# K of the last four head pairs: transposed by the DMA crossbar instead of TensorE

## Chip, cores, metric

One Trainium2 chip, one core. The metric is the device time of one execution in microseconds (us), lower is better. Medians are over repeated executions; all executions quoted here were of the same (fast) state. A profiled span is about 1.7 us shorter than the device time of the same execution, so spans are compared with spans and times with times.

## The reference, cut

Attention with a selection of key chunks, then a gated MLP with a spatial mixing step. Batch 4, 8 heads, sequence 768, head size 64; float32 in and out.

```python
# attention: per head, chunks of 32 keys; upper bound of q.k per chunk from the chunk's min and max of K
ub     = sum_d max(q * k_min[chunk], q * k_max[chunk])     # [B, H, 768, 24], causal chunks only
top    = the 6 chunks with the largest ub
scores = q @ k.T / 8, masked to the chosen chunks and to j <= i
x      = softmax(scores) @ v                               # heads side by side: [4, 768, 512]
# MLP
h    = relu(x @ w_in);  u, v = halves of h
v    = layernorm(v);    v = w_spatial @ v + b_spatial
out  = (u * v) @ w_out                                     # [4, 768, 512]
```

## The kernel before

The 32 heads are worked as 16 pairs (`i` = 0 to 15), two heads side by side in the 128 partitions, so K of a pair is a 128 x 768 tile after transposition. All steps of all pairs and of the four MLPs are put on a list of "beats"; a scheduler of the language then orders each engine's instructions by their dependences. The MLP of one batch element runs interleaved with the attention of the next.

K takes this way. It is loaded for two pairs at once by GpSimd (POOL) into a tile `k` that has three buffers, transposed, reduced per chunk to max and min (`kmm`, on VectorE), and copied into the operand of the score matmuls (`kh`, on VectorE):

```python
def load_k(g, hi, xy=None):                       # pairs 2g and 2g+1
    ...
    tiles["k", g] = sb.tile([P, 2, NQT, 2, D], F16, tag="k", name="k", bufs=3)
    ...
    nc.gpsimd.dma_start(out=t[:, :, :, 1 - hi, :]..., in_=source(k, b, h, 2))

def k_transpose(self):
    if self.i < 16:                               # in this kernel: always
        self.kT = kT = ps_ml.tile([P, S], F16, tag="mlp", name="kTp")       # PSUM
        for t in range(NQT):                      # 6 blocks of 128 x 128
            nc.tensor.transpose(kT[:, t * P:(t + 1) * P], self.k[:, t], identity)
    else:
        self.kT = sb.tile([P, S], F16, tag="kT", name="kT", bufs=3)         # SBUF
        nc.sync.dma_start_transpose(out=self.kT.rearrange("d (t s) -> d t s", s=P),
                                    in_=self.k.rearrange("p t h d -> p (t h d)"))
def k_max(self):
    nc.vector.tensor_reduce(self.kmm[:, 0, :], self.kT..., op=Alu.max)
def k_operand(self, hi):
    copy(self.kh[hi][d0:d1], self.kT[d0:d1])      # nc.vector.tensor_copy
```

Four more things share queues with this. SyncE (SP) issues all the crossbar transposes: of the attention output (`xT<-x`), of the selected queries from pair 8 on (`a<-qs`), of the gated MLP rows (`gT<-g`), and the output stores. POOL issues all loads and also does the causal mask of the exponentiated scores (`e<-e`) that the values matmuls read:

```python
def triangle(self, hi):
    nc.gpsimd.affine_select(out=blk, in_=blk, compare_op=Alu.is_ge, fill=0.0, ...)   # on e
def values(self, hi, blocks, ...):
    mm(self.av[:, qi, :], lhsT=self.e[hi][:, c:c + P], rhs=self.v[hi][:, t, 0:D + 1], ...)
def normalise(self, hi):                          # frees the one accumulator of the values
    nc.vector.reciprocal(rec, self.av[:, :, D:D + 1])
    nc.vector.tensor_tensor(self.x16[:, :, hi, :], in0=self.av[:, :, 0:D], in1=rec..., op=Alu.mult)
```

SP and POOL each work through their instructions in order. An instruction that waits holds up all that stand behind it (below, a load of POOL that waited 13.06 us held up the mask behind it).

The softmax here doesn't subtract the row's maximum and nothing guards it: scores larger than these inputs give would overflow.

## Time and profile before

| | before |
|---|---|
| median, range | 208.66 us (208.53 to 208.81) |
| profiled span | 206.9 us |
| PE busy | 187.8 us, 91% |
| PE busy from 78 to 160 us | 82.0 of 82 us |
| last matmul starts | 202.63 us |

The page of the kernel before: busy time by engine, then rows of 40 slices of the span; each digit is the busy share of a slice in tenths, and PEclk the TensorE clock that was granted.

```profile
span 206.9 us, 5068 instructions
PE 187.8 (91%) x1922; PEld 115.1 (56%) x1922; DVE 154.5 (75%) x454; ACT 158.1 (76%) x326; POOL 80.5 (39%) x100
...
PE   0368999898899999999999999999999999999992
...
PEclk9999999999999999999999999999999999999999
```

From the twelfth slice on, TensorE is busy for 90% or more of each slice (9), up to the last one. The view of busy time by stretch says the same with more figures; after each engine's busy time stand its instructions, then the granted clock (1.00 is full), the DMA share and GB/s.

```profile
core 0: us, PE busy (x) PEld busy (x) DVE busy (x) ACT busy (x) POOL busy (x), PEclk, DMA share, GB/s
60.00:70.00 10.00, 9.73 (x119) 6.47 (x117) 9.75 (x31) 8.38 (x17) 3.92 (x5) 1.00 2.02 154
70.00:78.00 8.00, 7.65 (x93) 5.23 (x93) 7.24 (x27) 7.22 (x18) 5.47 (x6) 1.00 1.50 103
78.00:83.00 5.00, 5.00 (x50) 2.95 (x48) 4.97 (x11) 4.79 (x12) 1.33 (x2) 1.00 3.58 128
...
100.00:130.00 30.00, 30.00 (x310) 17.73 (x307) 26.56 (x83) 26.83 (x61) 6.62 (x7) 1.00 1.09 143
```

So a TensorE instruction that is taken away between 78 and 160 us should be a gain, and a wait of TensorE put in there should be a loss that nothing later gives back.

The timeline of POOL (start, duration, then what it is; in brackets the idle time before it and what ended it):

```profile
59.65 2.09 POOL L327 DMA_DIRECT2D k<-in_k_dram  x2
61.69 0.94 POOL L278 TENSOR_SCALAR_AFFINE_SELECT e<-e 128x768 f16<-128x768 f16 x1
66.06 0.86 POOL L278 TENSOR_SCALAR_AFFINE_SELECT e<-e 128x768 f16<-128x768 f16 x1 [3.44 <-ACT e L271]
...
76.43 2.02 POOL L327 DMA_DIRECT2D k<-in_k_dram  x2 [1.80 <-PE kTp L170]
```

The K load of pairs 12 and 13 is issued at 59.65 us; the last one, of pairs 14 and 15, at 76.43 us, when TensorE has transposed the K that lay in the buffer (`kTp`). The mask of pair 5's second head, at 66.06 us, stands between them. TensorE needs that mask at 70.44 us, when it loads it as weights (timeline of the weight loads):

```profile
70.44 0.44 PEld L289 LDWEIGHTS <-e 128*128 128x128 f16 x6
```

The removed work itself, from the query for the tile `kTp` (duration min/median/max in ns, then first and last start):

```profile
L170 PE MATMUL kTp<-identity,k x96: 216/219/314, 5.7 to 135.9; 128*128 128x128 f16 x96
L194 DVE COPY kh<-kTp x30: 508/556/562, 15.8 to 140.9; 64x768 f16<-64x768 f16 x30
L178 DVE TENSOR_REDUCE kmm<-kTp x16: 924/953/958, 6.6 to 136.2; 128x24 f16<-128x768 f16 x16
```

One transpose takes 219 ns from start to end, but they are pipelined and start 55 ns apart, and that is what one costs a full TensorE.

### The profile page before, as it was taken

What the parts mean: (1) busy time and instruction counts of PE and PEld (TensorE: products, weight loads), DVE (VectorE), ACT (ScalarE), POOL (GpSimd) and SP (SyncE); (2) the same over time, 40 slices, a digit from 0 to 9 for tenths busy, and PEclk for the clock granted to TensorE, in tenths of its full rate; (3) what the DMA queues carried; (4) which work ended last, traced back from release to release, by engine and by line L of the source; (5) the groups of instructions that cost most, each with busy time, mean ns of one, the idle gap of its engine ahead of it and who ended that gap; (6) DMA issues with size and microseconds to landing.
All of it is one profiled execution on the core that took longest, in us unless ns stands there. A gap on an engine that the chain in (4) does not pass through costs nothing.

```text
span 206.9 us, 5068 instructions
## 1 busy us (share of the span) xinstructions
PE 187.8 (91%) x1922; PEld 115.1 (56%) x1922; DVE 154.5 (75%) x454; ACT 158.1 (76%) x326; POOL 80.5 (39%) x100
## 2 busy tenths in 40 slices
PE   0368999898899999999999999999999999999992
PEld 0266776775666665656655656565555454444440
DVE  6467979989799989899797999887647456365520
ACT  4797989899998889785989996669999830666042
POOL 7997659596992463236114111111111110000000
PEclk9999999999999999999999999999999999999999
DMA  5999999999999999979998926648782124540356
GB/s 38 92 118 154 140 178 158 173 177 167 177 162 162 97 119 128 135 130 147 149 278 153 180 62 57 127 88 158 181 166 65 38 29 92 187 152 3 72 128 256
DMA packets 114424, 27.27 MB, mean 132 GB/s; under 512 B 109536, under 2 KB 110816, under 8 KB 114400
## 3 DMA queue, kind: packets, MB, share of 16 engines
q0 software_dynamic: 76544, 12.20, 89.8%
q1 hardware_dynamic: 37856, 14.75, 36.4%
q8 instruction: 15, 0.25, 0.5%
q14 instruction: 9, 0.07, 0.1%
HBM read 24.38 MB, written 6.29 MB: 148 GB/s over the span
## 4 chain that ended last, share of the span: by engine, by line
PE 69%; ACT 17%; DVE 8%; issue 2%; DMA 2%; POOL 0%; DVEq 0%; ACTq 0%; POOLq 0%
PE mlp L388 40%; PE sc L266 12%; ACT e L271 10%; PE acc L289 7%; PE kTp L170 2%; ACT a L257 2%; DVE kmm L178 2%; PE ub L222 2%; DMA k<-in_k_dram 2%; PE trm L251 2%; ACT vraw L398 1%; PE tr L205 1%; DVE vn L412 1%; DVE kmm L182 1%; ACT u L420 1%
## 5 line engine op out<-in xcount | busy, mean ns | idle before, releaser
L271 ACT ACTIVATE e<-sc 128x512 f16<-128x512 f32 x192 | 96.9, 553 | 14.8 <-PE sc L266 13.4
L266 PE MATMUL sc<-a,kh 128*128 128x512 f16 (+3 forms) x256 | 65.5, 308 | 2.1 <-ACT e L271 1.5
L388 PE MATMUL mlp<-w_in_sb,xT 128*128 128x512 f16 x192 | 53.0, 379 | 0.1
L278 POOL TENSOR_SCALAR_AFFINE_SELECT e<-e 128x768 f16<-128x768 f16 x24 | 20.9, 869 | 66.3 <-ACT e L271 66.3
L289 PEld LDWEIGHTS <-e 128*128 128x128 f16 x672 | 31.4, 97 | 17.0 <-DVE x L297 3.8
L388 PE MATMUL mlp<-vn,wsT 128*128 128x512 f16 x144 | 37.3, 379 | 0.0
L289 PE MATMUL acc<-vt,e 128*128 128x65 f16 x672 | 35.3, 193 | 0.7 <-DVE x L297 0.4
L266 PEld LDWEIGHTS <-kh 128*128 128x128 f16 x256 | 22.7, 98 | 13.3 <-issue 0.8
L437 ACT COPY o<-mlp 128x512 f32<-128x512 f32 x24 | 14.1, 586 | 19.5 <-PE mlp L388 19.1
L400 DVE BATCH_NORM_STATS2 stats<-vraw 128x6 f32<-128x512 f32 x24 | 16.6, 693 | 12.9 <-ACT vraw L398 12.5
L388 PE MATMUL mlp<-w_out_sb,gT 128*128 128x512 f16 x96 | 25.1, 379 | 0.0
L388 PEld LDWEIGHTS <-xT 128*128 128x128 f16 x192 | 17.2, 97 | 12.6 <-issue 0.4
L427 DVE SCALAR_TENSOR_TENSOR g<-mlp,b_col,u 128x512 f16<-128x512 f32 x24 | 17.9, 748 | 7.3 <-PE mlp L388 6.2
L232 DVE MAX8 max<-ub 128x8 f32<-128x8 f32 (+4 forms) x160 | 15.6, 165 | 5.1 <-PE ub L222 4.9
L388 PEld LDWEIGHTS <-wsT 128*128 128x128 f16 x144 | 12.9, 98 | 10.4
L178 DVE TENSOR_REDUCE kmm<-kTp 128x24 f16<-128x768 f16 x16 | 15.2, 948 | 3.7 <-PE kTp L170 2.7
L297 DVE TENSOR_TENSOR x<-acc,rec 128x384 f16<-128x384 f32 x32 | 17.6, 551 | 0.4
L336 POOL DMA_DIRECT2D qs<-in_q_dram x14 | 14.6, 1049 | 5.9 <-PE sc L266 5.9
L194 DVE COPY kh<-kTp 64x768 f16<-64x768 f16 x30 | 16.5, 549 | 0.5
L398 ACT ACTIVATE vraw<-mlp 128x512 f32<-128x512 f32 x24 | 14.4, 601 | 3.0 <-PE mlp L388 3.0
L420 ACT ACTIVATE u<-mlp 128x512 f16<-128x512 f32 x24 | 14.3, 598 | 1.7 <-PE mlp L388 1.5
L327 POOL DMA_DIRECT2D k<-in_k_dram x14 | 14.4, 1045 | 2.5 <-PE kTp L170 1.8
(67 smaller groups left out, 230.2 us busy)
## 6 DMA issues: line engine op xcount, KB each, us to landing
out_dram<-o SPq DMA_DIRECT2D x24, 256.0 KB, 2.3
vt<-in_v_dram POOLq DMA_DIRECT2D x8, 384.0 KB, 8.8
k<-in_k_dram POOLq DMA_DIRECT2D x14, 192.0 KB, 8.1
qs<-in_q_dram POOLq DMA_DIRECT2D x14, 192.0 KB, 7.5
ws_raw<-in_moe_w_spatial_dram POOLq DMA_DIRECT2D x6, 192.0 KB, 6.9
w_in_sb<-in_moe_w_in_dram POOLq DMA_DIRECT2D x8, 128.0 KB, 6.9
w_out_sb<-in_moe_w_out_dram POOLq DMA_DIRECT2D x4, 128.0 KB, 7.9
k<-in_k_dram POOLq DMA_DIRECT2D x4, 96.0 KB, 3.4
```

The lines of the kernel that those rows point to most:

```text
L178: nc.vector.tensor_reduce(self.kmm[:, 0, :], self.kT.rearrange("d (c ch) -> d c ch", ch=CHUNK), axis=AX.X, op=Alu.max)
L194: copy(self.kh[hi][d0:d1], self.kT[d0:d1])
L266: mm(sc[:, col:col + n], lhsT=self.kh[hi][:, t * P:(t + 1) * P], rhs=self.a[:, q0 // P:(q0 + n) // P, hi, :], start=True, stop=not diag)
L271: nc.scalar.activation(out=self.e[hi][:, g * 512:g * 512 + width], in_=sc[:, 0:width], func=Act.Exp, scale=scale)
L278: nc.gpsimd.affine_select(out=blk, in_=blk, compare_op=Alu.is_ge, fill=0.0, base=0, channel_multiplier=-1, pattern=[[0, NQT], [1, P]])
L289: mm(self.av[:, qi, :], lhsT=self.e[hi][:, c:c + P], rhs=self.v[hi][:, t, 0:D + 1], start=first and n == 0, stop=last and n == len(blocks) ...
L297: nc.vector.tensor_tensor(self.x16[:, :, hi, :], in0=self.av[:, :, 0:D], in1=rec.to_broadcast([P, NQT, D]), op=Alu.mult)
L388: mm(st[group][:, 0:cols], lhsT=lhsT, rhs=rhs, start=(j == 0), stop=(j == n - 1))
L398: nc.scalar.activation(st["vraw"][:, ti, :], h, func=Act.Relu)
L400: nc.vector.bn_stats(stats, st["vraw"][:, ti, :])
L420: nc.scalar.activation(st["u"][:, ti, :], h, func=Act.Relu)
L427: nc.vector.scalar_tensor_tensor(g, in0=vs, scalar=b_col[:, ti:ti + 1], in1=st["u"][:, ti, :], op0=Alu.add, op1=Alu.mult)
```

## The change

The intent is to take 24 transposes (four pairs of six) off the engine that bounds the kernel, and to give them to the crossbar of the DMA path, which the kernel already uses for three other transpositions. The branch was in the code already; only its limit moves.

```diff
         def k_transpose(self):
-            if self.i < 16:
+            if self.i < 12:
                 self.kT = kT = ps_ml.tile([P, S], F16, tag="mlp", name="kTp")
                 for t in range(NQT):
                     nc.tensor.transpose(kT[:, t * P:(t + 1) * P], self.k[:, t], identity)
```

## The prediction

> **What bounds the kernel now.** From about 76 us to the last matmul at 202.7 us TensorE streams without gaps: the table by stretches has PE busy 10.00 of 10 us nearly everywhere, and matmuls start as fast as their columns allow (216 ns per 512 columns, 55 ns per 128-column transpose). All start-to-start slack from 80 us on adds up to about 1.6 us. Before 76 us ScalarE, VectorE and the loads share the limit (DMA 99% busy in the page's slices).
>
> **What the change removes.** 24 PE transposes, in four groups at 104.06, 114.76, 125.06 and 135.65 us (timeline): 24 x 55 ns = 1.3 us of a saturated PE. On VectorE the K copies (556 ns from PSUM) may get cheaper; the reductions (950 ns) hardly. VectorE is not the limit there.
>
> **What it adds.** Four crossbar transposes on the SP queue: by the like xT<-x transposes 1.2 us of issue, 2.7 us to landing on a quiet queue, over 8 us on a full one.
>
> **What it moves.** This decides it. The instruction order of the two built programs differs before 104 us. The K transposes are no longer tied to PE's place in the program, so the scheduler puts those of pairs 12, 13 and 14 on SP directly behind the first xT transpose (60.87 us before), and the last K load (pairs 14, 15) now reuses the buffer of pairs 12, 13. On POOL its first half is queued ahead of the triangle mask that ran at 66.06 us before, and it waits for both crossbar transposes of pairs 12 and 13. Those wait for the K load that lands at 70.96 us (issued 60.67, 10.3 us). The Trainium skill, "DMA: Bandwidth & Descriptors", section "Anatomy of one DMA", says that DMA engines do not wait on semaphores, the issuing sequencer does; this trace agrees (POOL sat idle 1.80 us before the K load at 76.43, until kTp).
>
> So, estimated from these durations: load landed 71.0; two transposes issued to 73.5, second landed about 75.0; POOL issues the load (1.03 us), masks (0.87 us): done about 77.0. PE loads its weights from that masked tile at 70.44 us in the old trace and runs in order: a hole of about 6.6 us, against a PE that is full afterwards.
>
> SP then holds up the transpose of pair 14, and behind it xT and the first A transpose, until about 82 us. A should land near 91 us; PE needs it at 87.14 + 6.6 = 93.8, so no second hole.
>
> **Clock.** The skill, "TensorE: Matmul & The Clock Gate", Part 1, says that an idle window of about 3.4 us halves the clock and a busy one restores it. Here early transposes start 107 ns apart, later ones 55 ns, which agrees. I add 1.7 us (0 to 3.4).
>
> **Sum.** 208.7 + 6.6 + 1.7 - 1.3 - 0.7 (slack between 70 and 76 us absorbed) = 215.0 us. Range 211.5 to 218. Chances: faster 0.04, same 0.13, slower 0.83.
>
> **What would show it.** PE idle 5 to 8 us near 70 to 77 us, its weight load (values, acc<-vt,e) released by the POOL mask; POOL idle there, released by the DMA kT<-k; slices of PEclk below 9 just after; first xT then three kT on SP, the third near 82 us; no kTp group after 95 us; PE gapless from about 85 us to the end, that stretch about 1.3 us shorter.
>
> **What would make it wrong.** The K load landing earlier, or quicker transposes: a smaller hole. A clock that stays up. A late A transpose: a second hole near 90 us. If POOL doesn't block, 207.4 us.

## The result

| | before | change |
|---|---|---|
| median, range | 208.74 us (208.53 to 209.19), 4 runs | 218.75 us (217.92 to 219.71), 4 runs |
| ratio, 95% interval | | 1.048 (1.0448 to 1.0513): slower |
| profiled span | 206.9 us | 217.0 us |
| mean granted clock | 1.000 | 0.974 |
| last matmul starts | 202.63 us | 212.28 us |

Ratios here and below are the mean time of one kernel's fast runs over that of the other's of the same rounds on the same chip, so not quite the ratio of the medians.

The page of the change:

```profile
span 217.0 us, 5030 instructions
PE 189.6 (87%) x1898; PEld 115.1 (53%) x1898; DVE 155.6 (72%) x454; ACT 158.7 (73%) x326; POOL 80.4 (37%) x100
...
PE   0479998988999069999999899999999999999992
...
PEclk9999999999999658999999999999999999999998
```

There is one slice in which TensorE is idle (0), and the clock falls with it (6, 5, 8). PE's busy time even rises, though it has 24 instructions fewer, since matmuls at half clock last longer. The same stretches as before:

```profile
60.00:70.00 10.00, 9.73 (x119) 6.49 (x117) 9.75 (x31) 8.37 (x17) 2.55 (x3) 1.00 1.99 159
70.00:78.00 8.00, 1.21 (x14) 0.72 (x14) 0.81 (x3) 1.20 (x3) 2.39 (x3) 0.66 0.37 57
78.00:83.00 5.00, 5.00 (x34) 3.08 (x32) 3.81 (x8) 3.02 (x8) 3.96 (x5) 0.53 1.91 122
...
100.00:130.00 30.00, 28.23 (x286) 16.10 (x284) 29.05 (x85) 25.37 (x58) 10.00 (x10) 1.00 1.36 163
```

Three losses can be read here. Up to 70 us TensorE does the same. From 70 to 78 us TensorE does 14 matmuls in place of 93. From 78 to 83 us it is "busy" but does 34, in place of 50, at a clock of 0.53. And from 100 to 130 us it does 286 in place of 310, with VectorE now at 29.05 of 30 us. (The change runs some 10 us late there, so the stretch doesn't hold the same work in both; that TensorE is busy for 28.23 us and no longer for 30.00 is the safer sign.)

**The hole.** POOL in the change, timeline:

```profile
59.58 2.09 POOL L327 DMA_DIRECT2D k<-in_k_dram  x2
61.61 0.94 POOL L278 TENSOR_SCALAR_AFFINE_SELECT e<-e 128x768 f16<-128x768 f16 x1
75.61 1.03 POOL L327 DMA_DIRECT2D k<-in_k_dram  x1 [13.06 <-DMA kT<-k]
76.64 0.88 POOL L278 TENSOR_SCALAR_AFFINE_SELECT e<-e 128x768 f16<-128x768 f16 x1
```

The last K load now stands ahead of the mask and waits for the crossbar transposes of pairs 12 and 13, whose buffer it reuses. POOL sits idle for 13.06 us, and the mask comes at 76.64 instead of 66.06 us. SP in the change, timeline; the line with x3 spans three issues, at 70.63, 71.90 and 81.70 us, with landings at 73.41, 74.75 and 88.19 us:

```profile
60.84 1.77 SPq L305 DMA_TRANSPOSE xT<-x  x1
70.63 12.29 SPq L173 DMA_TRANSPOSE kT<-k  x3
82.97 1.40 SPq L305 DMA_TRANSPOSE xT<-x  x1
```

The first of them waited for the load of K, which was issued at 60.59 and landed at 70.55 us. And the weight loads of TensorE:

```profile
70.14 0.15 PEld L388 LDWEIGHTS <-xT 128*128 128x128 f16 x2
77.58 0.35 PEld L289 LDWEIGHTS <-e 128*128 128x128 f16 x6 [7.28 <-POOL e L278]
```

So the chain is: K load landed, two transposes on SP, K load on POOL, mask on POOL, TensorE. Measured by the starts of the matmuls, the hole adds 6.95 us at 70.41 us.

**The clock.** The records of the granted clock show 0.5 from 72.50 to 82.74 us, in all 10.24 us. Of these about 5.2 us lie after the hole, with TensorE at work at half speed: a loss of about 2.6 us in this execution, worked out from those times.

**Later gaps.** From 100 us on there are new holes in TensorE's stream, of 0.40, 0.33, 1.15 and 0.54 us (105.18, 116.30, 120.84 and 127.81 us). Each stands before a values matmul that waits for the accumulator, that is for VectorE's normalisation (`x`). VectorE in the change around the largest, timeline:

```profile
116.70 0.94 DVE L178 TENSOR_REDUCE kmm<-kT 128x24 f16<-128x768 f16 x1
...
118.16 0.93 DVE L182 TENSOR_REDUCE kmm<-kT 128x24 f16<-128x768 f16 x1
...
120.38 0.18 DVE L296 RECIPROCAL rec<-acc 128x6 f32<-128x6 f32 x1
120.59 1.10 DVE L194 COPY kh<-kT 64x768 f16<-64x768 f16 x1
121.61 0.53 DVE L297 TENSOR_TENSOR x<-acc,rec 128x384 f16<-128x384 f32 x1
```

A K copy of 1.10 us stands between the reciprocal and the product of one normalisation, and TensorE waits for the product. With `kT` ready early, the work on K of pairs 12 to 15 is no longer held back by TensorE, and stands earlier and closer together in VectorE's order. The kernel before has no such gap between 74 and 160 us.

What the K work costs from its new place, from the query for the tile `kT`:

```profile
L194 DVE COPY kh<-kT x8: 331/358/1096, 102.5 to 138.2; 64x768 f16<-64x768 f16 x8
L173 SPq DMA_TRANSPOSE kT<-k x4: 1214/1240/1282, 70.6 to 115.7; - x4
L178 DVE TENSOR_REDUCE kmm<-kT x4: 931/936/952, 110.9 to 125.0; 128x24 f16<-128x768 f16 x4
```

The copies take 358 ns instead of 556 at the median, but three of the eight took 820, 1005 and 1096 ns. Each of these three ran while POOL was at work on a mask or a load issue, and ended 0.15 to 0.22 us after POOL's instruction, while the other five met no instruction of POOL (the 1096 ns one at 121.69 us, after a load issue from 120.11 to 121.54 us). That one held up the other is read from these times; no run separates it. The reductions hardly differ (936 and 953 ns); this agrees with the Trainium skill, "VectorE: DVE Perf Modes", section "Rules for kernel authors", which says to expect no faster mode from a `tensor_reduce`.

### The profile page after: what moved, and what is told of

It is laid out like the page before. It is cut to its first block, busy times and chain, and to the rows that moved or that the text cites. A ratio compares the mean times of both kernels' runs of the same rounds, so it can differ in the third digit from the quotient of the medians.

```text
span 217.0 us, 5030 instructions
## 1 busy us (share of the span) xinstructions
PE 189.6 (87%) x1898; PEld 115.1 (53%) x1898; DVE 155.6 (72%) x454; ACT 158.7 (73%) x326; POOL 80.4 (37%) x100
## 4 chain that ended last, share of the span: by engine, by line
PE 58%; ACT 13%; DVE 12%; DMA 7%; POOL 4%; issue 3%; SPq 1%; POOLq 0%; ACTq 0%; DVEq 0%
PE mlp L388 34%; PE sc L266 10%; ACT e L271 8%; PE acc L289 6%; DMA k<-in_k_dram 6%; DVE kmm L178 2%; DVE x L297 2%; DVE kmm L182 2%; PE ub L222 1%; PE trm L251 1%; DMA kT<-k 1%; DVE vn L412 1%; PE kTp L170 1%; ACT km L189 1%; DVE max L232 1%
## 5 line engine op out<-in xcount | busy, mean ns | idle before, releaser
L266 PE MATMUL sc<-a,kh 128*128 128x512 f16 (+3 forms) x256 | 66.2, 311 | 2.1 <-ACT e L271 1.5
L388 PE MATMUL mlp<-w_in_sb,xT 128*128 128x512 f16 x192 | 54.2, 384 | 0.1
L289 PE MATMUL acc<-vt,e 128*128 128x65 f16 x672 | 35.9, 195 | 8.9 <-POOL e L278 6.8
L296 DVE RECIPROCAL rec<-acc 128x6 f32<-128x6 f32 x32 | 5.9, 185 | 13.2 <-PE acc L289 13.1
L412 DVE TENSOR_SCALAR vn<-vraw,mv,rstd 128x512 f16<-128x512 f32 x24 | 13.1, 600 | 1.6 <-ACT rstd L410 1.6
```

Source lines behind the costliest of these rows:

```text
L266: mm(sc[:, col:col + n], lhsT=self.kh[hi][:, t * P:(t + 1) * P], rhs=self.a[:, q0 // P:(q0 + n) // P, hi, :], start=True, stop=not diag)
L388: mm(st[group][:, 0:cols], lhsT=lhsT, rhs=rhs, start=(j == 0), stop=(j == n - 1))
L412: nc.vector.tensor_scalar(st["vn"][:, ti, :], in0=st["vraw"][:, ti, :], scalar1=st["mv"][:, ti, 0:1], scalar2=st["rstd"][:, ti, :], op0=Al ...
```

## The experiments

Two theories were held against each other. **Theory A**: the crossbar transpose as such is harmless; what costs is where it stands in the in-order queues of SP and POOL and which buffers it keeps, so that TensorE waits, loses its clock, and meets a reordered VectorE. **Rival B**: four more crossbar transposes cost time wherever they stand (SP issue, DMA traffic, slower neighbours). All kernels gave the right result, except e10. Its output is wrong, which doesn't matter for the time. "Before" is the kernel before on the same chip.

| run | median (range), us | ratio to before (95%) |
|---|---|---|
| e1_kbuf4 | 210.91 (209.86 to 211.76) | 1.011 (1.0065 to 1.0154) |
| e2_only_12_13 | 220.00 (219.53 to 220.47) | 1.054 (1.0523 to 1.0558) |
| e3_only_14_15 | 214.84 (213.89 to 216.18) | 1.0305 (1.026 to 1.035) |
| e4_warm | 217.21 (216.40 to 217.93) | 1.0413 (1.0384 to 1.0442) |
| e5_behind_xT4 | 217.25 (216.59 to 218.36) | 1.0416 (1.0382 to 1.0449) |
| e6_behind_xT5 | 213.16 (212.81 to 213.54) | 1.0215 (1.0199 to 1.0231) |
| e7_kbuf4_act | 210.06 (209.75 to 211.46) | 1.0079 (1.0043 to 1.0115) |
| e8_before_kbuf4 | 208.41 (208.16 to 208.66) | 0.999 (0.9973 to 1.0007) |
| e9_placed | 212.11 (210.36 to 212.71) | 1.0143 (1.0105 to 1.0182) |
| e10_no_transpose | 208.38 (208.05 to 208.79) | 0.9988 (0.9973 to 1.0003) |
| e11_kbuf4_pin | 207.92 (207.62 to 210.35) | 0.9992 (0.9953 to 1.0031) |
| e12_change_again | 219.11 (218.44 to 220.10) | 1.0503 (1.0468 to 1.0539) |
| e13_warm_again | 217.04 (216.71 to 217.69) | 1.0404 (1.0376 to 1.0432) |
| e14_change_pin | 218.02 (217.33 to 218.43) | 1.0444 (1.0417 to 1.0471) |
| e15_warm_pin | 215.92 (214.50 to 216.50) | 1.0324 (1.0283 to 1.0365) |

The chips differed: e1 to e4 ran on one, e5 to e8 on a second, e9 to e11 on a third, e12 to e15 on a fourth. The kernel before took 208.57, 208.63, 208.74 and 208.64 us there.

### e1: a fourth buffer for K

With four buffers the last K load reuses nothing that a crossbar transpose still reads, so POOL doesn't have to wait for SP. The transposes stay where they are on SP.

```diff
-            tiles["k", g] = sb.tile([P, 2, NQT, 2, D], F16, tag="k", name="k", bufs=3)
+            tiles["k", g] = sb.tile([P, 2, NQT, 2, D], F16, tag="k", name="k", bufs=4)
```

> The change, with a fourth buffer for the K loads, so that the last K load waits for no transpose. Theory (the buffer reuse stalls POOL, POOL stalls PE for 7 us, the clock drops): POOL masks the first tile behind the two last K loads near 66 us again, PE has no hole near 70 to 77 us, the clock stays at 1.00, and 207.4 to 209.8 us, where the spread is what VectorE's new order costs between 100 and 130 us (2.3 us of new PE gaps in the changed kernel). Rival (the crossbar traffic itself, or reading K from SBUF, is what is slow): still 215 us or more.

Measured: 210.91 us, 1.1 us above the expected range and 4 us below the rival's. The hole at 70 us is gone and the clock stays at 1.0. POOL of e1, timeline:

```profile
63.42 2.05 POOL L327 DMA_DIRECT2D k<-in_k_dram  x2 [0.87 <-DMA vt<-in_v_dram]
65.80 0.86 POOL L278 TENSOR_SCALAR_AFFINE_SELECT e<-e 128x768 f16<-128x768 f16 x1 [0.34 <-ACT e L271]
```

The mask is back at 65.80 us. About eight of the ten lost microseconds come from this one wait and what follows from it. What is left is seen in the profiled execution (211.76 us, the slowest of the four): 3.0 us are two gaps, at 86.66 us (1.20, scores wait for the first A transpose, which SP issued at 82.04 and not at 77.96 us) and at 95.84 us (1.77, a mask stood on POOL behind a Q load that was held up). The VectorE gaps of 1.15 and 0.54 us stay, at 114.19 and 121.16 us.

### e2 and e3: half of the change each

```diff
-            if self.i < 12:
+            if self.i not in (12, 13):     # e2: only pairs 12 and 13 by the crossbar
+            if self.i < 14:                # e3: only pairs 14 and 15 by the crossbar
```

> Half of the change: pairs 12 and 13 alone by the crossbar; these two feed the buffer that the last K load reuses. Theory: the hole of 7 us near 70 us and the clock drop are all there, 216 to 218.5 us. Rival (cost per crossbar transpose, of traffic or of SBUF reads): half of the loss, about 213.7 us.

Measured: 220.00 us, above the expected 216 to 218.5, with the hole at the same place, 8.58 us long. In this execution the K load landed at 71.96 us, 1.4 us later than in the change, and the transpose of pair 13 at 76.19 us. Pairs 12 and 13 alone make the whole loss, and somewhat more.

> The other half: pairs 14 and 15 alone. In the built order the last K load again reuses the buffer of pairs 8 and 9, so the theory expects no hole near 70 us and 207.5 to 209.5 us. Rival (cost per transpose): about 213.7 us.

Measured: 214.84 us, a miss: it should have been harmless, and cost 6.3 us. The hole at 70 us is gone, as expected, but a new one of 4.50 us opens at 95.40 us. SP of e3, and below it POOL, timeline:

```profile
86.43 2.54 SPq L173 DMA_TRANSPOSE kT<-k  x2
...
92.66 1.43 SPq L246 DMA_TRANSPOSE a<-qs  x1
```

```profile
97.14 2.04 POOL L336 DMA_DIRECT2D qs<-in_q_dram  x2 [8.98 <-DMA a<-qs]
99.17 0.88 POOL L278 TENSOR_SCALAR_AFFINE_SELECT e<-e 128x768 f16<-128x768 f16 x1
```

Two K transposes on SP, which wait there until their K load has landed at 86.36 us, push the A transpose of pair 9 from 86.90 (before) to 92.66 us. It reads `qs`, which the next Q load on POOL overwrites; POOL waits 8.98 us for it, and the mask behind that load waits too. It is the same mechanism with other names: an in-order SP, a reused buffer, an in-order POOL, a mask, TensorE. What failed in the expectation was that only one such knot was looked for. The losses of the halves (11.4 and 6.3 us) don't add up to that of the whole (10.0 us), so neither is a price per transpose.

### e4: keep TensorE occupied during the hole

120 matmuls of 122 columns into unused PSUM columns are put before the values that wait, so that TensorE isn't idle for long.

```diff
+            if self.i == 5 and hi == 1 and last:
+                for _ in range(120):
+                    mm(self.bank[:, NQT * (D + 1):512], lhsT=identity, rhs=tri[:, 0:122], start=False, stop=False)
             for n, (t, qi) in enumerate(blocks):
```

> The change, with 120 matmuls of 122 columns (about 53 ns each, 6.4 us) into unused columns of the accumulator's bank directly in front of the weight load that waits for POOL: the hole stays, but PE is busy in it. If the drop of the clock to half (72.5 to 82.7 us in the profile of the changed kernel) costs time by itself, the clock stays at 1.00 and the time falls by about 2.6 us, to 216.1 us. If the clock costs nothing beyond the hole, 218.7 us; if the filler itself gets in the way, more.

Measured: 217.21 us, 1.5 us below the change, where 2.6 had been expected; the clock records show 1.0 throughout, up to the tail. The hole stayed (the values started at 78.42 us). As the hole differed between chips, this couldn't be set against the change cleanly; e12 to e15 do that.

### e5 and e6: the K transposes later on SP

Each K transpose is ordered behind the xT transpose of the pair four (e5) or five (e6) before it.

```diff
+                with tc.issue_after(pairs[self.i - 4].xt.ins):        # e6: self.i - 5
                     nc.sync.dma_start_transpose(out=self.kT..., in_=self.k...)
```

> All four pairs by the crossbar, but each K transpose is queued on SP behind the xT transpose of the pair four before it, about the place in the program where PE did it. In the built order POOL's queue and the reuse of the K buffer are then as in the kernel before. Theory: no hole near 70 us, none near 95 us, clock 1.00. But the transposes of pair 12 would be issued near 105.8 us and land near 109 us, while VectorE's order asks for it at 104.6 us, so VectorE waits some 4 us and PE may get a hole of 0 to 4 us near 107 us: 207.5 to 211.5 us. Rival (each crossbar transpose costs 2 us by itself): 215 us or more.

> As e5, but behind the xT transpose of the pair five before: issued near 93.7, 105.8, 113 and 124 us, landing some 4 us later, before VectorE asks for them. Theory: no hole near 70 or 95 us, clock 1.00; the 1.3 us of PE transposes are won and up to 1.5 us of PE gaps between 100 and 130 us remain, since VectorE still takes some reductions earlier than before: 207.3 to 208.9 us, the first version not slower than the kernel before. Rival (cost per transpose): 215 us or more.

Measured: 217.25 and 213.16 us, both misses. There is no hole at 70 us. But now `kT` comes too late for the place that VectorE's order gives it. VectorE of e5, timeline:

```profile
108.49 0.95 DVE L179 TENSOR_REDUCE kmm<-kT 128x24 f16<-128x768 f16 x1 [4.02 <-DMA kT<-k]
...
109.96 0.18 DVE L297 RECIPROCAL rec<-acc 128x6 f32<-128x6 f32 x1
...
110.46 0.55 DVE L298 TENSOR_TENSOR x<-acc,rec 128x384 f16<-128x384 f32 x1
```

VectorE stands still for 4.02 us, the normalisation behind the reduction waits with it, and TensorE has a gap of 3.58 us at 107.27 us, after which the clock is 0.5 for 3.41 us. Later waits of VectorE for `kT` (1.85, 0.68 and 2.28 us) and what follows from them give TensorE four more gaps up to 146 us, 3.8 us in sum. In e6 the wait is 2.59 us and the gap 2.50 us, and another gap of 1.20 us, at 105.89 us, waits for an A transpose. Both theories had left out how far a late transpose is passed on by VectorE's order. The number of e5 is one that rival B had forecast (215 or more); it is the gaps and what released them that speak for theory A here, and e11 below that decides.

### e7 and e8: e1 with its copies elsewhere, and a control

e7 is e1 with the K copies of pairs 12 to 15 on ScalarE; e8 is the kernel before with the four buffers of e1.

```diff
-            copy = nc.scalar.copy if self.i < 1 else nc.vector.tensor_copy                     # e7
+            copy = nc.scalar.copy if self.i < 1 or self.i >= 12 else nc.vector.tensor_copy
```

> e1 (fourth K buffer), with the copies of K from the transposed tile on ScalarE instead of VectorE for the last four pairs. In e1 PE had gaps of 0.35, 1.15 and 0.54 us at 109 to 121 us in front of values matmuls that wait for VectorE's normalisation; one of the copies took 1.10 us instead of 0.36 there. If VectorE's load and that slow copy make these gaps, they shrink to under 1 us in sum and the time falls by about 1 us to 210 us or less, unless ScalarE (8.7 of 10 us busy there) now gives gaps of its own. If VectorE is not their cause, they stay.

> Control: the kernel before with a fourth K buffer and nothing else. The last K load can go out some 12 us earlier, among other loads. Theory: nothing waits on it, 208.2 to 209.5 us; if the early load alone delays the first A transpose, as in e1 (PE gap of 1.2 us near 87 us), up to 210 us.

Measured: 210.06 and 208.41 us. In e7 the VectorE gaps become smaller (0.30 and 0.77 us), and others appear that wait for an A transpose (0.70 us) and for ScalarE (0.38 and 0.33 us). In e8 nothing moves, so the fourth buffer is no gain by itself, and e1's gain over the change is the removed wait.

### e9: transposes placed by hand, VectorE's order pinned

The K transposes of pairs 12 and 13 are ordered behind the A transpose of pair 9, those of 14 and 15 behind that of pair 10; `kT` gets four buffers; and VectorE's work on K is pinned to its old places (the "pin": max behind the previous pair's last top-8, min behind its selection, copies behind the min).

```diff
+            with behind(self.i >= 12 and pairs[self.i - 1].last_top):
+                self.kmax = nc.vector.tensor_reduce(self.kmm[:, 0, :], ...)
+            with behind(self.i >= 12 and pairs[self.i - 1].picked):
+                self.kmin = nc.vector.tensor_reduce(self.kmm[:, 1, :], ...)
+            with behind(self.i >= 12 and self.kmin):
+                copy(self.kh[hi][d0:d1], self.kT[d0:d1])
```

> All four transposes by the crossbar, placed by hand: on SP those of pairs 12 and 13 behind the A transpose of pair 9, those of 14 and 15 behind that of pair 10 (four kT buffers), so that they land well before they are read; on VectorE the reductions and copies of K queued where they stood in the kernel before. The built orders of POOL and ScalarE are as before. Theory (all of the loss is queue order and what it makes wait): no PE gap over 0.6 us after 76 us, clock 1.00, 1.3 us won: 207.3 us, between 206.9 and 208.3. Rival (crossbar transposes or K in SBUF cost something by themselves): over 209 us although the orders are as before.

Measured: 212.11 us, a miss, and again a number that the rival had forecast (over 209). All the gaps that wait for the normalisation are gone, but one of 2.63 us is there at 98.15 us. SP of e9 around it, and VectorE, timeline:

```profile
90.04 3.32 SPq L177 DMA_TRANSPOSE kT<-k  x2
93.45 1.43 SPq L437 DMA_TRANSPOSE gT<-g  x1
```

```profile
100.19 0.75 DVE L434 SCALAR_TENSOR_TENSOR g<-mlp,b_col,u 128x512 f16<-128x512 f32 x1 [2.98 <-DMA gT<-g]
```

Here the K transposes stood in the way of the gT transposes; VectorE waited 2.98 us for a buffer of `g`, and TensorE for VectorE. The six executions of e9 fall into two groups: two with a mean clock of 1.000 took 210.36 and 210.44 us, four with 0.987 to 0.992 took 211.94 to 212.71 us. The profiled one is of the second group: after its gap the clock is 0.5 for 3.41 us.

### e10: no transposition at all (wrong result on purpose)

K is used untransposed, with VectorE pinned. This is the bound of what the change could win: neither the crossbar nor TensorE does the work.

```diff
-                self.kT = sb.tile([P, S], F16, tag="kT", name="kT", bufs=3)
-                nc.sync.dma_start_transpose(out=self.kT..., in_=self.k...)
+                self.kT = self.k.rearrange("p t h d -> p (t h d)")
```

> Wrong result on purpose: the last four pairs use K untransposed in place of its transpose, so PE loses the 24 transposes and nothing else is added; VectorE pinned as in e9. It measures the most that the change can win. Theory: 24 x 55 ns = 1.3 us, so 207.3 us (207.0 to 207.7). If PE were not the limit there, 208.6 us; if freeing PSUM banks helps beyond the transposes, under 207.

Measured: 208.38 us, about 0.3 us below before, where 1.3 had been expected. No new gap from 78 to 195 us, and the last matmul starts at 201.50 us, 1.13 us earlier than before; yet the span is only 0.5 us shorter. At the end two gT transposes landed 4.14 and 3.52 us after their issue instead of about 2.45, VectorE waited 1.70 us for `g`, TensorE got a gap of 0.49 us, and the last store landed 2.67 us after issue instead of 2.04. (In e11 below it is much the same: 3.70, 3.18 and 2.72 us.) Why those landings took longer is not shown by the runs. What is shown is that even free transposes hardly shorten this kernel. (As a bound it is good to some tenths only: most executions of e11, below, are still a little faster.)

### e11: the fourth buffer and the pin

e1 with the pin of e9 and nothing else: the crossbar transposes stay at their early place on SP.

```diff
-            tiles["k", g] = sb.tile([P, 2, NQT, 2, D], F16, tag="k", name="k", bufs=3)
+            tiles["k", g] = sb.tile([P, 2, NQT, 2, D], F16, tag="k", name="k", bufs=4)
+            ... the pin of e9 ...
```

> e1 (transposes early on SP, fourth K buffer) with VectorE's order pinned as in e9 and nothing else. It tells the two kinds of gaps in e1 apart. Theory: the gaps of 0.35, 1.15 and 0.54 us at 109 to 121 us come from VectorE's order and vanish; those of 1.20 us near 87 us and 1.77 us near 96 us come from the A transposes held up on SP and stay: 210.9 - 2.0 = 208.9 us (208.3 to 209.6). If VectorE's order is not the cause, 210.9 us.

Measured: 207.92 us, below the expected range of 208.3 to 209.6: the VectorE gaps vanished as expected, but those near 87 and 96 us, which were to stay, are gone too. SP of e11, timeline:

```profile
71.54 4.71 SPq L176 DMA_TRANSPOSE kT<-k  x3
...
78.91 3.20 SPq L252 DMA_TRANSPOSE a<-qs  x1
```

The stream of TensorE has no gap that it hadn't before, and its last matmul starts at 201.45 us. All four K transposes run on the crossbar, so rival B falls: they cost no measurable time when no in-order queue passes a wait on. Of six executions four took 207.62 to 207.96 us, two 209.60 and 210.35 us. The slow two were not profiled. In the profiled one the first A transpose was issued at 78.91 us and landed at 85.42 us, just in time; in e1 it was issued 3.1 us later, and cost a gap. The pin orders VectorE alone; in e1 the loads and transposes in front of it had landed later, and why is not shown. That the slow two had the same is likely, but not shown. Over all six the ratio is 0.9992 (0.9953 to 1.0031), so no version here beats the kernel before for certain.

### e12 to e15: clock and VectorE order, on one chip

The change again (e12), with e4's filler (e13), with the pin (e14), and with both (e15), to size two terms that had been read only from traces of different chips. The edits are those shown with e4 and e9.

> The changed kernel itself, on the same chip as the three runs that follow. Expected 217.9 to 219.7 us: PE hole of 6.9 to 8.6 us near 70 us, clock 0.5 for about 10 us after it, later PE gaps with VectorE as releaser of about 2.4 us in sum.

> Filler matmuls keep TensorE occupied during the hole. Clock theory: the hole stays, the clock stays 1.0, and this comes out 2.3 to 2.9 us below the change of the same chip. If the half clock were mere bookkeeping (the rival), the time stays within 0.7 us of the change.

> The change with its VectorE order pinned to that of before (reductions and copies of K of pairs 12 to 15 in their old places). VectorE-order theory: hole and half clock stay, the later gaps vanish, 1.8 to 2.6 us below the change of the same chip. Rival: those later gaps only follow from the hole, and stay (time within 0.7 us of the change).

> Both at once. If the two terms are separate they add: about 4.6 us below the change of the same chip, that is before plus hole (7 to 8.6 us) minus 0.5 to 1.3 us minus slack 0.7: 213.8 to 216 us. If they overlap, the saving is nearer to the larger of the two alone.

Measured: 219.11, 217.04, 218.02 and 215.92 us. The filler saves 2.07 us without the pin and 2.10 with it; the pin saves 1.09 us without the filler and 1.12 with it. The two terms are separate and add, as far as four executions of each can tell: those of one kernel lie 1.0 to 2.0 us apart, so each saving is uncertain by half a microsecond to one. Together they save 3.2 us, where 4.6 had been expected. Busy time by stretch, first e12, then e13, then e14:

```profile
70.00:85.00 15.00, 7.71 (x81) 5.00 (x81) 6.17 (x23) 6.42 (x15) 7.23 (x7) 0.77 1.10 89
100.00:130.00 30.00, 28.32 (x287) 16.15 (x286) 29.09 (x84) 25.42 (x59) 9.87 (x10) 1.00 1.41 162
```

```profile
70.00:85.00 15.00, 13.74 (x211) 11.26 (x209) 9.30 (x30) 6.93 (x16) 7.16 (x7) 1.00 1.14 91
```

```profile
100.00:130.00 30.00, 30.00 (x313) 17.87 (x312) 25.89 (x81) 26.83 (x60) 10.04 (x10) 1.00 1.43 172
```

With the filler the clock is 1.00 where it was 0.77. With the pin TensorE is full again from 100 to 130 us (30.00 in place of 28.32) and VectorE is back at 25.89 us. The trace of e12 shows gaps of 0.42, 1.15 and 0.53 us there, 2.1 us in sum, but the pin won only about 1.1 us. The profiled execution of e14 had its half clock for 10.24 us, that of e12 for 6.83 us; the spans of single traces therefore don't subtract cleanly. The expected 1.8 to 2.6 us for the pin was a miss by size, if the medians are taken. But both profiled pinned executions were already 0.5 to 0.6 us late when they entered the hole, before any pinned instruction ran (last matmul before it at 71.03 us in e14 against 70.40 in e12, 70.72 in e15 against 70.21 in e13). Counted from the end of the hole to the last matmul, and at full clock in both, e15 is 1.78 us shorter than e13 (131.11 against 132.89 us). So the VectorE term may be nearer to 1.8 than to 1.1 us; more executions would have to tell. The clock term came out a little below the expected 2.3 to 2.9 us; e13 has a gap of 0.91 us at 113.41 us, where TensorE, being earlier, now waits for an A transpose.

What is left in e15, 7.28 us over before, is about the size of the hole: 7.4 us on this chip (e12, e14).

## Why the prediction was right or wrong

The direction, the place and the main mechanism, the chain of waits that makes the hole, were right; a second mechanism was left out. The time was not right: 10.0 us were lost, 6.3 had been forecast, and 218.75 lies outside the range of 211.5 to 218.

- **The hole** ("a hole of about 6.6 us"): right. 6.95 us in the profiled change, 7.4 on the chip of e12. The chain of waits was as forecast, step by step: load landed at 70.55 (71.0 forecast), second transpose at 74.75 (75.0), mask done at 77.5 (77.0). The page "DMA: Bandwidth & Descriptors", section "Anatomy of one DMA", that the sequencer waits and not the DMA engine, is borne out by the 13.06 us that POOL stood still. e1 shows the cause: without that wait the time is 210.91 us.
- **The second hole that wasn't to come** ("no second hole"): right, though with less room than forecast. A of pair 8 landed at 93.30 us (91 forecast), and TensorE did not wait for it.
- **The clock** ("I add 1.7 us, 0 to 3.4"): right in kind, a little small. It is worth 2.1 us, give or take half a microsecond (e13 against e12, e15 against e14). The page "TensorE: Matmul & The Clock Gate", Part 1, gives an idle window of about 3.4 us in a free-running watch; the records agree on the step (half clock for 10.24, 6.83 or 3.41 us), and on the free running: the clock fell only about 2 us after the last matmul before the hole in one execution (70.41 to 72.50 us), and 3.6 us after it in another (70.40 to 74.03 us in e12). So a whole window without work was not needed here.
- **VectorE** ("VectorE is not the limit there", "PE gapless from about 85 us to the end"): this step failed. The prediction took VectorE's order as given. It had noticed that K transposes are no longer tied to TensorE's place in the program, and followed that on SP and POOL, but not on VectorE, which was at 26.56 of 30 us and is also in order. The term was left at 0; it measures 1.1 us by the medians (e14, e15), and perhaps 1.8 by the traces.
- **The gain** ("24 x 55 ns = 1.3 us of a saturated PE", counted in full): this step failed too. The last matmul does come 1.13 us earlier when the transposes are merely left out (e10), but the time falls by about 0.3 us in e10, and by 0.9 us in the better four of six executions of e11. A full TensorE until 202.63 us isn't the end of the kernel; in e10 the tail of gT transposes and stores behind it took most of the gain.
- **Absorbed slack** ("0.7 us"): 0.44 us, the gap at 73.97 us of the kernel before, which the hole swallowed.

The sum with measured terms is 7.2 (hole, between the two chips) + 2.1 + 1.1 - 0.4, less 0.3 to 0.9 for the gain, that is 9.1 to 9.7 us, against 10.0 measured in the result and 10.5 in e12. With 1.8 us for VectorE it would be 9.8 to 10.4. What is left was not assigned. Of the 3.7 us that the forecast lacked, 1.1 (or 1.8) are VectorE's order, 0.4 to 1.0 the gain, 0.6 the hole, 0.4 the clock and 0.3 the slack. The missing VectorE term is the largest of the steps that failed; the others are terms of the right kind and too small a loss (or too large a gain), all to the same side. The forecast's "If POOL doesn't block, 207.4 us" was too simple as well: e1 doesn't block, and takes 210.91 us, since SP and VectorE pass their own waits on.

## What to carry to other kernels

Before an instruction is moved to a queue that works in order, list what stands behind it there, which buffers it keeps and who reuses them: here a transpose that cost no measurable time by itself (e11) held back a load, the load held back a mask, and the mask held back the engine that was to be relieved. A dependence that is removed also frees the scheduler on engines that the change doesn't touch; compare the order on every engine that is nearly full (VectorE was at 26.56 of 30 us here), and pin it where it was good. And ask first what the bound is worth: a kernel with the work simply left out (e10) shows in one run that about 0.3 us was to be had (0.9 us in the better executions of e11).

## What the Trainium skill lacked or had wrong

- "VectorE: DVE Perf Modes", section "The three transpose paths", gives 1309 ns for 128 x 128 on the DMA crossbar and 390 ns on TensorE. It lacks the two figures that decide such an exchange: in a full stream a TensorE transpose costs 55 ns (six take 0.50 us from the first start to the last end, one alone 219 ns; for plain matmuls of 128 columns the skill has this spacing on another page), and a crossbar transpose of 128 x 768 takes 1.21 to 1.28 us of SP's queue and 2.8 to 6.5 us to landing in the change. The measured figures decide here; the page's own were not tried in isolation.
- "SBUF — State Buffer", section "SBUF: two separate sides", says that VectorE in a two-port mode and GpSimd lock each other out for a whole instruction. The trace of the change agrees: K copies from SBUF took 358 ns at the median, but 820, 1005 and 1096 ns in the three cases where GpSimd was at a mask or at a load issue (that the copies ran in a two-port mode, the trace doesn't show). The section says that either side can be the one that waits; its warning is about the DMA that is held up. It lacks the case met here: a load issue of 1.43 us on GpSimd beside a VectorE copy three times as long, ahead of an instruction that TensorE waits for.
- "TensorE: Matmul & The Clock Gate", Part 1, under "HAM oscillation", counts half of the throttled time as lost. Here only the throttled time in which TensorE has work counts: half of the whole record of 10.24 us would be 5.1 us, half of 6.83 us 3.4 us; the runs show 2.1 between the medians. And the idle window of about 3.4 us need not be idle as a whole. The changes of the clock in these traces lie a multiple of 3.41 us apart; worked out from TensorE's busy time in the windows that these steps mark off, the clock fell after windows with 1.86 us (change) and 2.23 us (e9) idle, and stayed up after one with 1.47 us (e1); the border lies near 1.86 us, since e14 stayed up after as much near its end. It came back after a window with 0.55 us idle (e12), and not after one with 1.36 us (e14). Where the end of the hole fell in its window thus made the half clock 6.83 us long in one and 10.24 us in the other, after holes of nearly the same length (7.38 and 7.44 us) on one chip.
- No page has that a wait for a DMA transpose can be handed on over two in-order queues (SP and GpSimd) by the reuse of a buffer; it cost 7 us here and 4.5 us in e3.
